# Decay slopes and small sums moved to PSUM, k products in one bank, and the group sums' transfers at other chunks

## Chip, core and metric

The kernel runs on one core of a Trainium2 chip. The metric is the device time in microseconds of one execution. Before the change it is 184.69 us, the median of 3 runs (184.53 to 184.96). The profile comes from one further execution with the hardware profiler on.

## What is computed

Two blocks over the same 2048 rows of 448 features, mixed by a gate. Block A is linear attention with 16 heads of 28, block B a long convolution with kernels made from 256 complex exponentials per feature.

```python
x = A_x                                            # (1, 2048, 448)
g = sigmoid((x * gate_w).sum(-1, keepdims=True))

def A(x, wqkv, wo):
    q, k, v = heads(x @ wqkv)                      # 16 heads of 28
    phi = lambda t: where(t > 0, t + 1, exp(t)) + 1e-6
    pq, pk = phi(q), phi(k)
    kv = einsum("bhsd,bhse->bhde", pk, v)
    z = einsum("bhsd->bhd", pk)
    o = einsum("bhqd,bhde->bhqe", pq, kv) / (einsum("bhqd,bhd->bhq", pq, z)[..., None] + 1e-6)
    return merge(o) @ wo

def B(u, ...):
    dt = exp(log_dt); A = -exp(log_A_real) + 1j * A_imag
    C = (C_real + 1j * C_imag) * dt[:, None]
    K = 2 * einsum("dn,dnl->dl", C, exp(A * dt * arange(L))).real
    return causal_conv(u, K) + u * D_skip          # by FFT in the reference

out = g * A(x) + (1 - g) * B(x)
```

For the inputs of this case every feature passes a test (`okc`) by which K is flat enough over the sequence that the convolution is a running sum of x times one slope per feature, called `near`. A general path (`general_conv`) stands behind a branch and is not taken.

## The kernel before, in words

The 2048 rows are 16 chunks of 128 rows (`NC = 16`); chunk c has its turned rows (for products that contract over features) and its plain rows. Every product in full precision is made of products of high and low parts: a ScalarE copy rounds to the high part, and a subtraction on GpSimd or VectorE (`low`, line 243) gives the low part. TensorE's work per chunk in the main loop (lines 509 to 566, c = 2 to 13) is, in order:

- `project(c + 1)` with wk: 11 matmuls into one PSUM bank (line 341), the k product of the *next* chunk. The banks are tags: it goes to `k` for odd c and to `v1` for even c, so it alternates;
- `project(c)` with wq: 11 matmuls into bank `q`;
- `do_g(c)`: 11 matmuls that add x-transposed times phi(k) into four banks g0 to g3 (line 416);
- in chunks 5, 7, 9 and 11 `group_heads` (line 442): two matmuls with a triangle matrix `tri` that turn a group's row sums into running sums, into bank `v0`. In 7, 9 and 11 they stand between blocks 2 and 3 of `do_g`, in 5 behind it.

The k product is turned into phi(k) by `k_feature` (ScalarE L367, L368, VectorE L369), `k_high` (ScalarE L373) and `k_low` (VectorE L379 twice: the low part and the running z); the last two read the PSUM bank. The q product goes through `q_post`: ScalarE L387 and, up to chunk 5, L356, then VectorE L357 and L360; from chunk 6 on ScalarE L391 to L393, then VectorE L394. Bank `q` is free for the next chunk after the last of these.

The convolution works on four groups of four chunks. `group_load` (L423, on SP's queue) loads a group into its home: group 0 into `wvo[:, 1]`, group 1 into the end of `pq`, which first holds the operands of the slopes and so must wait until L298 and L299 have read them, groups 2 and 3 into `room` and `spare`. `running_a` (L427) and `running_b` (L431) are accumulating transfers within SBUF that GpSimd issues: together they make running sums over the four rows of a partition; `running_b` reads what `running_a` wrote. `group_split` (ScalarE L435, GpSimd `low`) takes high and low part of the group's last row for `group_heads`. `convolve` (L447, L448, two chunks at a time, c from 6 on) adds the heads, which are in PSUM, and multiplies by `near`. `group_add` (L454) adds the group into y by another accumulating transfer of GpSimd. `skip` (L259, GpSimd) is the term u times D_skip.

`s4d_prepare` (lines 286 to 321) makes the slopes from the parameters in six steps, which the loop calls by `steps`: exponentials in chunk 1's step, row sums (L297, L298 on ScalarE, L299 on VectorE) in chunks 2 and 3, the small sums of 112 x 4 (L303 to L316, VectorE) in chunk 4, and in chunk 5 four transposes that spread the slopes over all partitions, with a ScalarE copy (L321) to `near` in SBUF.

The order of work on each engine is the order of the program; nothing is reordered. SP issues the loads in program order too, and an issue that waits holds those behind it. `load_x(c + 3)` (L207) at the head of chunk c loads the chunk three ahead, into one of four buffers.

After the loop, the last chunk's products, the head products (`kv_products`, which read wv in `wvo[:, 0]`) and the output products follow.

Of the kernel before, what the change touches and what calls it, by code (L numbers as in the profile page):

```python
# [7 lines left out]
F32 = mybir.dt.float32  # L8
F32R = mybir.dt.float32r
I32 = mybir.dt.int32  # L10
AF = mybir.ActivationFunctionType
ALU = mybir.AluOpType
# [3 lines left out]
P = 128  # L16
S = 2048
D = 448
# [4 lines left out]
J = 4  # L23
# [9 lines left out]
QW = 512  # L33
EDGE = 16
G = 4
SMALL = 2.0 ** -70
FLAT = 2.0 ** 35
BIG = 3.4028234e38
# [107 lines left out]
def gated_mix_kernel(ctx: ExitStack, tc: tile.TileContext, xin, wq_d, wvo_d, abc_d, ldt_d, dsk_d,  # L146
# [26 lines left out]
    gcr = const.tile([UZ, RX], F32R, name="gcr")  # L173
    ones = const.tile([P, P], F32R, name="ones")
    rows = const.tile([P, S], F32, name="rows")
    near, dsk = (rows[:, i * D:(i + 1) * D] for i in range(2))
    u = const.tile([UZ, D], F32, name="u")
    zb = const.tile([P, D], F32, name="zb")
    ldt = const.tile([DJ, J], F32, name="ldt")
# [34 lines left out]
    o = 0  # L214
# [32 lines left out]
        ACT.copy(w[:, :NAT], turned[c])  # L247
        low(POOL, w[:, NAT:], turned[c], w[:, :NAT])

    def split_n(c):  # L250
        r, w = plain[c], xn_p.tile([P, NX], F32R, name="xn", tag="n")
        xn[c] = w
        ACT.copy(w[:, :XC - NAT], r)  # L253
        low(POOL, w[:, XC - NAT:], r[:, :D], w[:, :D])
        if c > 2:
            skip(c)

    def skip(c):
        POOL.tensor_tensor(out=y[:, c], in0=plain[c][:, :D], in1=dsk, op=ALU.mult)  # L259
# [22 lines left out]
    def small():  # L282
        cnt[0] += 1
        return sm[:, cnt[0] - 1]

    def s4d_prepare():
        tt = lambda eng, o, a, b, op: eng.tensor_tensor(out=o, in0=a, in1=b, op=op)
        stt = lambda o, a, k, b, op1: DVE.scalar_tensor_tensor(out=o, in0=a, scalar=k, in1=b, op0=ALU.mult, op1=op1)
        junk = [yf[:DJ, F0 + (i - 2) * 2 * N:F0 + (i - 1) * 2 * N].rearrange("p (i n) -> p i n", i=2) for i in range(2)]
        s0, s1, dt, am, p0, p1, d2, md, b0, b1 = (small() for _ in range(10))  # L290
        for j in range(J):
            ACT.activation(abc[:, 0, j], abc[:, 0, j], AF.Exp)
        ACT.activation(dt, ldt, AF.Exp)
        tt(DVE, d2, dt, dt, ALU.mult)
        yield
        for j in range(J):
            ACT.activation(junk[0], abc[:, 0:2, j], AF.Square, accum_out=am[:, j:j + 1])  # L297
            ACT.activation(junk[0][:, 0], abc[:, 2, j], AF.Copy, accum_out=s0[:, j:j + 1])  # L298
            DVE.scalar_tensor_tensor(out=junk[1], in0=abc[:, 2:4, j], scalar=1.0, in1=abc[:, 0:2, j], op0=ALU.mult,  # L299
                                     op1=ALU.mult, accum_out=s1[:, j:j + 1])  # L300
            if j % 2:
                yield
        tt(DVE, md, am, d2, ALU.mult)  # L303
        stt(p0, s0, 2.0, dt, ALU.mult)
        stt(p1, s1, -2.0, d2, ALU.mult)
        DVE.tensor_scalar(out=md, in0=md, scalar1=SMALL, scalar2=None, op0=ALU.is_le)
        stt(b0, p0, -1.0, p0, ALU.max)
        stt(b1, p1, -1.0, p1, ALU.max)
        yield
        DVE.tensor_scalar(out=p0, in0=p0, scalar1=-BIG, scalar2=BIG, op0=ALU.max, op1=ALU.min)  # L310
        DVE.scalar_tensor_tensor(out=md, in0=b0, scalar=1.0 / FAR, in1=md, op0=ALU.is_ge, op1=ALU.mult)
        stt(okc, b1, FLAT, b0, ALU.is_le)
        DVE.scalar_tensor_tensor(out=md, in0=b0, scalar=FAR, in1=md, op0=ALU.is_le, op1=ALU.mult)
        tt(DVE, okc, okc, md, ALU.mult)
        tt(DVE, p0, p0, okc, ALU.mult)
        DVE.tensor_reduce(out=oks, in_=okc, op=ALU.add, axis=AX.X)  # L316
        yield
        o = ps.tile([P, 512], F32, name="p", tag="v0")
        for j in range(J):
            PE.transpose(o[:, j * DJ:(j + 1) * DJ], p0[:, j:j + 1].to_broadcast([DJ, P]), ident[:DJ, :DJ])  # L320
        ACT.copy(near, o[:, :D])  # L321

    def pieces(c, wh, wl, n, tag, last=None):
        o = ps.tile([P, 512], F32, name=tag, tag=tag)
# [20 lines left out]
    def project(*args, **kw):  # L345
        o, run = pieces(*args, **kw)
        run(11)
        return o
# [22 lines left out]
    def k_high(c):  # L371
        pkh[c] = tp.tile([P, 512], F32R, name="pkh", tag="pkh")[:, EDGE:EDGE + D]
        ACT.add(pkh[c], pks[c], 1e-6)  # L373
# [34 lines left out]
    def do_g(c, blocks=range(4)):  # L408
        w = xn[c]
        for i in blocks:  # L410
            a = w[:, 64 + i * P:64 + (i + 1) * P]
            b = w[:, XC - NAT + 64 + i * P:][:, :P] if i < 3 else None
            seq = [(a, pkh[c]), (a, pkl[c]), (b, pkh[c])] if i < 3 else \
                  [(a, pkh[c]), (a[:, :64], pkl[c])][::1 if c == 0 else -1]
            for n, (a, b) in enumerate(seq):
                PE.matmul(g[i][:a.shape[1], :D], lhsT=a, rhs=b, start=c == 0 and n == 0,  # L416
                          stop=c == NC - 1 and n == len(seq) - 1)
# [4 lines left out]
    def group_load(g):  # L422
        SP.dma_start(out=homes[g], in_=xin[g * G:(g + 1) * G, :, NAT:LO].rearrange("r p d -> p r d"))  # L423

    def running_a(g):
        w = homes[g]
        POOL.dma_start(out=w[:, 1::2], in_=w[:, 0::2], accum_op=ALU.add)  # L427

    def running_b(g):
        w = homes[g]  # L430
        POOL.dma_start(out=w[:, 2:], in_=w[:, 1:2].to_broadcast([P, 2, D]), accum_op=ALU.add)  # L431

    def group_split(g):
        w = sums[g] = tp.tile([P, 2, D], F32R, name="sums", tag="v0", bufs=1)
        ACT.copy(w[:, 0], homes[g][:, G - 1])  # L435
        low(POOL, w[:, 1], homes[g][:, G - 1], w[:, 0])

    def group_heads(g):
        o = heads[g] = ps.tile([P, 512], F32, name="v", tag="v0")[:, :D]
        w = sums.pop(g)  # L440
        for i in range(2):
            PE.matmul(o, lhsT=tri, rhs=w[:, i], start=i == 0, stop=i == 1)

    def convolve(c):
        g, i = c // G, c % G
        a, full = homes[g][:, i:i + 2], [P, 2, D]
        DVE.tensor_tensor(out=a, in0=a, in1=heads[g][:, None, :].to_broadcast(full), op=ALU.add)  # L447
        DVE.tensor_tensor(out=a, in0=a, in1=near[:, None, :].to_broadcast(full), op=ALU.mult)  # L448
        if i and g < NC // G - 1:
            for k in (g, UL + g):  # L450
                SP.dma_start(out=u[k:k + 1], in_=homes[g][P - 1:P, G - 1])
# [40 lines left out]
    for j in (2, 3, 0):  # L492
# [11 lines left out]
    skip(0)  # L504
    split_n(3)
    woh, wol = [], []
    pieces_at = {3: [(running_a, 0)], 4: [(running_b, 0)], 5: [(running_a, 1)], 6: [(running_b, 1), (running_a, 2)],
                 8: [(running_b, 2), (running_a, 3)], 10: [(running_b, 3)]}
    for c in range(2, NC - 2):
        if c + 3 < NC:  # L510
            load_x(c + 3)
        if c == 2:
            SP.dma_start(out=cst, in_=cst_d)
        if c == 4:
            SP.dma_start(out=wvo[:, 0], in_=wvo_d[:, 0])
        if c == 10:
            SP.dma_start(out=wo, in_=wvo_d[:DJ, 1])
        if c in (2, 4, 5, 7):
            group_load(c // 2 - (c < 5))
        ko = project(c + 1, wkh, wkl, D, "k" if c % 2 else "v1")  # L520
        if c > 5:
            convolve(2 * c - 12)
        split_t(c + 2)
        for f, k in pieces_at.get(c, ()):
            f(k)
        if c > 5:
            split_n(c + 2)
        k_feature(c + 1, ko)
        if c in (5, 7, 9, 11):
            group_split(c // 2 - 2)  # L530
        k_high(c + 1)
        k_low(c + 1)
        qo = project(c, wqh, wql, D + 2, "q")
        q_post(c, qo)
        if c < 5:
            steps(2 if c == 4 else 1)
        if c == 3:
            DVE.tensor_copy(tri, trir)
            DVE.tensor_copy(gcr, gcat)
        if c == 7:  # L540
            SP.dma_start(out=okr[:, None, :DJ], in_=oks[:, None, :])
        if c == 9:
            DVE.tensor_reduce(out=okr[:, DJ:], in_=okr[:, :DJ], op=ALU.add, axis=AX.X)
            DVE.tensor_copy(okn, okr[:, DJ:])
        do_g(c, (0, 1))
        if c == 5:
            steps(1)
        do_g(c, (2,))
        if c in (7, 9, 11):
            group_heads(c // 2 - 2)  # L550
        do_g(c, (3,))
        if c == 5:
            group_heads(0)
        if c < 4:
            skip(c - 1)
        if c < 6:
            split_n(c + 2)
        if c in (7, 9, 11, 13):
            group_add(c // 2 - 3)
        for j in {12: (0, 1), 13: (2, 3)}.get(c, ()):  # L560
            w = xn_p.tile([P, NX], F32R, name="wo", tag="n") if j < 2 else xp.tile([P, XC], F32R, name="wo", tag="xr")
            w = w[:DJ, :2 * D].rearrange("p (i d) -> p i d", i=2)
            woh.append(w[:, 0])
            wol.append(w[:, 1])
            ACT.copy(woh[j], wo[:, j])
            low(POOL, wol[j], wo[:, j], woh[j])
# [402 lines left out]
```

## Time and profile before

| | |
|---|---|
| median of 3 runs | 184.69 us |
| profiled execution | 185.1 us |
| its span in the trace | 183.2 us |
| TensorE busy | 166.5 us, 852 matmuls |
| VectorE busy | 130.4 us |
| ScalarE busy | 105.9 us |
| GpSimd busy | 123.2 us |
| mean granted TensorE clock | 0.987 |

The span runs from the first to the last instruction of the trace; the execution's time has 1.9 us around it. In rows of a timeline the columns are start and duration in us, engine (PE is TensorE, DVE VectorE, ACT ScalarE, POOL GpSimd, SP the queue that issues loads), line, operation, output and input, shapes, and in brackets the idle time before and what ended it. Rows of waits read: engine and line, what it waited for, us in total, how often, the longest. Rows of a line's instructions give durations in ns as least, median and most. In rows of a stretch (such as 54.00:58.00) come its length, the busy time of TensorE, its weight loads, VectorE, ScalarE and GpSimd, the granted clock, and the transfers' share and GB/s. A row that begins with an output and an input alone is one of DMA issues: count, size, us to landing.

### The profile page before, as it was taken

Reading aid. Unit: us, or ns where it says so; the run is one execution under the profiler, and the core shown is the slowest. Engines: PE = TensorE matmul, PEld = TensorE weight load, DVE = VectorE, ACT = ScalarE, POOL = GpSimd, SP = SyncE. Lnnn points to the kernel's source line nnn. Section 1 sums busy time; section 2 is a strip of 40 time slices with the busy share of each in tenths; the row PEclk is TensorE's granted clock in tenths of the full one; section 3 lists DMA queues with packets and bytes.
Section 4 is the critical chain, followed back from the end, with each engine's and each line's share of the span. In section 5 each row is a group of like instructions: output and inputs, shape, how many; then the busy total and the mean of one; then the engine's idle time right before and its main releaser. Section 6 shows DMA issues by size and latency. Waiting matters only on the chain.

```text
span 183.2 us, 2706 instructions
## 1 busy us (share of the span) xinstructions
PE 166.5 (91%) x852; PEld 147.8 (81%) x852; DVE 130.4 (71%) x232; ACT 105.9 (58%) x241; POOL 123.2 (67%) x128
## 2 busy tenths in 40 slices
PE   7999999996907999898897799999999999999990
PEld 2798999995906999796896699998988999999990
DVE  0857548898809488782888568787889898997550
ACT  3779489846015663674727858656474555564441
POOL 6074776985708995778845976985959899773100
PEclk9999999999996999999999999999999999999998
DMA  6999968495999581989997480090031122122221
GB/s 186 415 305 265 245 193 302 166 236 172 275 293 336 151 141 25 176 264 236 279 225 134 140 179 0 0 194 8 1 67 52 52 101 104 50 101 101 102 95 62
DMA packets 12186, 29.45 MB, mean 161 GB/s; under 512 B 1549, under 2 KB 8410, under 8 KB 12170
## 3 DMA queue, kind: packets, MB, share of 16 engines
q1 hardware_dynamic: 9274, 21.81, 36.9%
q0 software_dynamic: 2752, 7.34, 21.6%
q8 instruction: 7, 0.11, 0.2%
q10 hardware_dynamic: 144, 0.11, 0.2%
q14 instruction: 9, 0.07, 0.1%
HBM read 17.93 MB, written 3.67 MB: 118 GB/s over the span
## 4 chain that ended last, share of the span: by engine, by line
PE 51%; DMA 20%; DVE 8%; ACT 8%; POOL 6%; issue 2%; SPq 1%; ACTq 0%; DVEq 0%; POOLq 0%
PE a L664 20%; DMA wvo<-wvo 10%; PE g L416 8%; PE v L341 7%; PE q L341 6%; DMA room<-room 5%; PE tr L638 4%; PE k L341 3%; DVE wvo L448 3%; DMA wvo<-in 3%; DVE room L448 2%; POOL xt L243 2%; DMA y<-in 2%; POOL y L259 2%; POOL xn L243 2%
## 5 line engine op out<-in xcount | busy, mean ns | idle before, releaser
L664 PE MATMUL a<-wk,th 128*128 128x448 f32 (+1 forms) x170 | 36.7, 361 | 0.1
L416 PE MATMUL g<-pkh,xn 128*128 128x448 f32 x112 | 35.7, 364 | 0.0
L664 PEld LDWEIGHTS a<-wk,th 128*128 128x128 f32 x170 | 29.4, 189 | 2.2 <-issue 0.3
L341 PE MATMUL q<-wqh,xt 128*128 128x450 f32 x120 | 27.8, 368 | 3.5 <-DVE pq L360 1.8
L243 POOL TENSOR_TENSOR xt<-xr,xt 128x512 fp32r<-128x512 f32 x14 | 21.2, 1515 | 14.2 <-ACT xt L247 14.2
L243 POOL TENSOR_TENSOR xn<-xr,xn 128x448 fp32r<-128x448 f32 x16 | 23.9, 1492 | 5.7 <-ACT xn L253 3.9
L341 PEld LDWEIGHTS q<-wqh,xt 128*128 128x128 f32 x120 | 22.3, 188 | 6.2 <-DVE pq L394 2.5
L416 PE MATMUL g<-pkl,xn 128*128 128x448 f32 x64 | 23.4, 366 | 0.0
L416 PEld LDWEIGHTS g<-pkh,xn 128*128 128x128 f32 x112 | 21.0, 188 | 2.2
L341 PE MATMUL v<-wk,xt 128*128 128x448 f32 x99 | 22.2, 374 | 0.0
L259 POOL TENSOR_TENSOR y<-xr,rows 128x448 f32<-128x448 f32 x16 | 21.8, 1365 | 0.0
L576 POOL TENSOR_TENSOR room<-pq,zb 128x448 f32<-128x448 f32 x16 | 18.6, 1168 | 3.6 <-issue 2.6
L341 PEld LDWEIGHTS v<-wk,xt 128*128 128x128 f32 x99 | 19.5, 197 | 1.5
L341 PE MATMUL k<-wk,xt 128*128 128x448 f32 x77 | 17.4, 368 | 0.1
L601 POOL TENSOR_TENSOR room<-pq,den 128x336 f32<-128x336 f32 x16 | 12.2, 763 | 7.4 <-ACT den L590 4.4
L341 PEld LDWEIGHTS k<-wk,xt 128*128 128x128 f32 x77 | 14.3, 187 | 1.8 <-ACT wk L464 0.4
L669 DVE SCALAR_TENSOR_TENSOR ot<-y,og,a 128x448 f32<-128x448 f32 (+1 forms) x17 | 10.7, 629 | 5.1 <-PE a L664 5.1
L646 DVE TENSOR_TENSOR th<-tr,th 128x512 fp32r<-128x512 f32 x16 | 11.0, 690 | 2.6 <-ACT th L645 2.0
L416 PEld LDWEIGHTS g<-pkl,xn 128*128 128x128 f32 x64 | 11.2, 174 | 1.2 <-DVE pkl L379 0.2
L645 ACT CAST th<-tr 128x512 fp32r<-128x512 f32 x16 | 9.4, 588 | 4.6 <-PE tr L638 4.4
L373 ACT ACTIVATE pkh<-v 128x448 fp32r<-128x448 f32 x9 | 4.9, 543 | 12.3 <-DVE v L369 12.3
L341 PE MATMUL q<-wql,xt 128*128 128x450 f32 x45 | 11.7, 365 | 0.0
(178 smaller groups left out, 326.8 us busy)
## 6 DMA issues: line engine op xcount, KB each, us to landing
xr<-in SPq DMA_DIRECT2D x15, 512.0 KB, 6.1
out<-ot SPq DMA_DIRECT2D x15, 224.0 KB, 1.9
pq<-in SPq DMA_DIRECT2D x4, 448.0 KB, 13.4
wvo<-in SPq DMA_DIRECT2D x2, 896.0 KB
y<-in SPq DMA_DIRECT2D x2, 480.0 KB, 3.7
y<-in SPq DMA_DIRECT2D x2, 450.0 KB, 7.8
wvo<-wvo POOLq DMA_DIRECT2D x2, 448.0 KB, 9.5
pq<-in SPq DMA_DIRECT2D x1, 896.0 KB, 5.3
```

Source lines behind the costliest of these rows:

```text
L243: eng.tensor_tensor(out=o, in0=r, in1=h.bitcast(F32), op=ALU.subtract)
L259: POOL.tensor_tensor(out=y[:, c], in0=plain[c][:, :D], in1=dsk, op=ALU.mult)
L341: PE.matmul(o[:, :n], lhsT=a, rhs=b, start=run.n == 1, stop=not seq)
L416: PE.matmul(g[i][:a.shape[1], :D], lhsT=a, rhs=b, start=c == 0 and n == 0, stop=c == NC - 1 and n == len(seq) - 1)
L448: DVE.tensor_tensor(out=a, in0=a, in1=near[:, None, :].to_broadcast(full), op=ALU.mult)
L576: POOL.tensor_tensor(out=pd[c], in0=pq[:, c], in1=zb, op=ALU.mult)
L601: POOL.tensor_tensor(out=n[:, :3, :DJ].rearrange("p j (h d) -> p j h d", h=4), in0=a, in1=r[:, :H - 4].rearrange("p (j h) -> p j h", j=3)[ ...
L638: PE.transpose(o[:, j * P:(j + 1) * P], n[:, j], ident)
L645: ACT.copy(h, ov)
L646: DVE.tensor_tensor(out=l, in0=ov, in1=h.bitcast(F32), op=ALU.subtract)
L664: PE.matmul(a[:, lo:hi], lhsT=u_, rhs=w_[:, lo:hi], start=n == 0, stop=n == 10)
L669: DVE.scalar_tensor_tensor(out=ot[:, lo:hi], in0=y[:, c, lo:hi], scalar=og[:, c:c + 1], in1=a[:, lo:hi], op0=ALU.mult, op1=ALU.add)
```

## The change

- Seven of the small tiles stay in SBUF (two of them second copies, `n0` and `n1`, of the products `p0` and `p1`); six lie in a PSUM bank, tag `v0`. The square of dt is made by ScalarE.
- The transposed slopes stay in PSUM, tag `v1`; the ScalarE copy L321 is gone, and L448 reads the bank.
- The k product goes to `v1` in chunks 2 and 4 and to `k` in all others, so that from chunk 5 on each one follows the last in the same bank.
- `group_load(0)` is issued ahead of the loop, those of groups 1, 2 and 3 at the end of chunks 3, 4 and 5 (before: heads of chunks 2, 4, 5 and 7). The load of wv goes from chunk 4 to chunk 11.
- `running_a` is issued at the end of chunks 2, 4, 5 and 6 (before: in chunks 3, 5, 6 and 8), `running_b` in chunks 4, 6, 7 and 9 (before: 4, 6, 8 and 10).
- `group_heads` stands behind all four blocks of `do_g`.
- From chunk 6 on `skip` stands behind `group_split` on GpSimd. The copies of `tri` and `gcr` go from VectorE in chunk 3 to ScalarE in chunk 4.

```diff
+PAIRS = (2, 4, 5, 6)
+HALVES = (4, 6, 7, 9)
...
-    near, dsk = (rows[:, i * D:(i + 1) * D] for i in range(2))
+    dsk = rows[:, D:2 * D]
+    near = []
...
-    def split_n(c):
+    def split_n(c, both=True):
...
-        if c > 2:
+        if c > 2 and both:
             skip(c)
...
-        s0, s1, dt, am, p0, p1, d2, md, b0, b1 = (small() for _ in range(10))
+        s0, s1, am, pn, b0, n0, n1 = (small() for _ in range(7))
+        o = ps.tile([P, 512], F32, name="sums", tag="v0")
+        dt, p0, p1, d2, md, b1 = (o[:DJ, i * J:(i + 1) * J] for i in range(6))
...
-        tt(DVE, d2, dt, dt, ALU.mult)
+        ACT.activation(d2, dt, AF.Square)
...
         stt(p0, s0, 2.0, dt, ALU.mult)
+        stt(n0, s0, 2.0, dt, ALU.mult)
         stt(p1, s1, -2.0, d2, ALU.mult)
+        stt(n1, s1, -2.0, d2, ALU.mult)
...
-        stt(b0, p0, -1.0, p0, ALU.max)
-        stt(b1, p1, -1.0, p1, ALU.max)
+        stt(b0, p0, -1.0, n0, ALU.max)
+        stt(b1, p1, -1.0, n1, ALU.max)
...
-        tt(DVE, p0, p0, okc, ALU.mult)
+        tt(DVE, pn, p0, okc, ALU.mult)
...
-        o = ps.tile([P, 512], F32, name="p", tag="v0")
+        o = ps.tile([P, 512], F32, name="p", tag="v1")
+        near.append(o[:, :D])
...
-            PE.transpose(o[:, j * DJ:(j + 1) * DJ], p0[:, j:j + 1].to_broadcast([DJ, P]), ident[:DJ, :DJ])
-        ACT.copy(near, o[:, :D])
+            PE.transpose(o[:, j * DJ:(j + 1) * DJ], pn[:, j:j + 1].to_broadcast([DJ, P]), ident[:DJ, :DJ])
...
-        DVE.tensor_tensor(out=a, in0=a, in1=near[:, None, :].to_broadcast(full), op=ALU.mult)
+        DVE.tensor_tensor(out=a, in0=a, in1=near[0][:, None, :].to_broadcast(full), op=ALU.mult)
...
-    pieces_at = {3: [(running_a, 0)], 4: [(running_b, 0)], 5: [(running_a, 1)], 6: [(running_b, 1), (running_a, 2)],
-                 8: [(running_b, 2), (running_a, 3)], 10: [(running_b, 3)]}
+    group_load(0)
     for c in range(2, NC - 2):
         if c + 3 < NC:
             load_x(c + 3)
...
-        if c == 4:
-            SP.dma_start(out=wvo[:, 0], in_=wvo_d[:, 0])
...
-        if c in (2, 4, 5, 7):
-            group_load(c // 2 - (c < 5))
-        ko = project(c + 1, wkh, wkl, D, "k" if c % 2 else "v1")
+        if c == 11:
+            SP.dma_start(out=wv, in_=wvo_d[:, 0])
+        ko = project(c + 1, wkh, wkl, D, "v1" if c in (2, 4) else "k")
...
-        for f, k in pieces_at.get(c, ()):
-            f(k)
+        if c in HALVES:
+            running_b(HALVES.index(c))
         if c > 5:
-            split_n(c + 2)
+            split_n(c + 2, False)
...
         if c in (5, 7, 9, 11):
             group_split(c // 2 - 2)
+        if c > 5:
+            skip(c + 2)
...
-        if c == 3:
-            DVE.tensor_copy(tri, trir)
-            DVE.tensor_copy(gcr, gcat)
+        if c == 4:
+            ACT.copy(tri, trir)
+            ACT.copy(gcr, gcat)
...
-        do_g(c, (2,))
-        if c in (7, 9, 11):
+        do_g(c, (2, 3))
+        if c in (5, 7, 9, 11):
             group_heads(c // 2 - 2)
-        do_g(c, (3,))
-        if c == 5:
-            group_heads(0)
         if c < 4:
             skip(c - 1)
         if c < 6:
             split_n(c + 2)
+        if c in (3, 4, 5):
+            group_load(c - 2)
+        if c in PAIRS:
+            running_a(PAIRS.index(c))
```

## Prediction

> **What bounds the kernel now.** I read the page first, then the waits of TensorE alone, then TensorE's timeline around its longest wait, and from there the timelines of the engines named as releasers.
>
> ```profile
> PE 166.5 (91%) x852; PEld 147.8 (81%) x852; DVE 130.4 (71%) x232; ACT 105.9 (58%) x241; POOL 123.2 (67%) x128
> ```
> ```profile
> PE v L442 <- ACT rows L321: 5.2, 1, 5.2
> PE q L341 <- DVE pq L360: 1.8, 1, 1.8
> PE q L341 <- DVE pq L394: 1.7, 2, 1.0
> PE v L442 <- POOL sums L243: 1.7, 2, 0.9
> ...
> PE v L442 <- ACT sums L435: 0.6, 1, 0.6
> ```
>
> TensorE is busy 91% of the span, and these five rows (waits in the main loop) are 11.0 us, nearly all that it idles once it has begun. After the last of them the chain that ended last is TensorE alone until the final stores, so a microsecond won in chunks 2 to 11 should reach the end. The change can win what these gaps hold; it cannot touch the rest.
>
> ```profile
> 37.21 1.77 PE L341 MATMUL q<-wqh,xt 128*128 128x450 f32 x8
> ...
> 41.62 2.37 PE L341 MATMUL k<-wk,xt 128*128 128x448 f32 x11
> 45.75 1.85 PE L341 MATMUL q<-wqh,xt 128*128 128x450 f32 x8 [1.77 <-DVE pq L360]
> ...
> 50.46 0.37 PE L416 MATMUL g<-pkh,xn 128*128 128x448 f32 x1
> 56.06 1.12 PE L442 MATMUL v<-sums,tri 128*128 128x448 f32 x2 [5.23 <-ACT rows L321]
> 56.97 3.32 PE L341 MATMUL v<-wk,xt 128*128 128x448 f32 x11
> ```
> ```profile
> 54.00:58.00 4.00, 1.94 (x5) 1.78 (x6) 2.77 (x5) 3.48 (x8) 2.54 (x3) 0.70 1.08 306
> ```
>
> The long gap costs more than 5.23 us: the granted clock from 54 to 58 us is 0.70, and the k product of chunk 7, 2.37 us elsewhere, takes 3.32. With about 0.5 us on the pair of L442 that is 1.4 us more. What ended it:
>
> ```profile
> 44.26 0.64 ACT L247 CAST xt<-xr 128x512 fp32r<-128x512 f32 x1
> ...
> 54.09 0.56 ACT L435 CAST sums<-wvo 128x448 fp32r<-128x448 f32 x1 [8.13 <-DMA wvo<-wvo]
> ...
> 55.47 0.54 ACT L321 COPY rows<-p 128x448 f32<-128x448 f32 x1
> ```
>
> ScalarE stood 8.13 us at the copy of group 0's sums, for the second accumulating transfer (L431), and the slopes' copy (L321) is queued behind it.
>
> **The other releasers** are late because VectorE stands still:
>
> ```profile
> L448 DVE TENSOR_TENSOR wvo<-wvo,rows x2: 1399/3178/4958, 58.4 to 66.2; 128x896 f32<-128x896 f32 x2
> ...
> L448 DVE TENSOR_TENSOR room<-room,rows x2: 1153/2643/4133, 90.5 to 99.2; 128x896 f32<-128x896 f32 x2
> ```
> ```profile
> L447 DVE TENSOR_TENSOR wvo<-wvo,v x2: 1077/1078/1078, 57.2 to 65.1; 128x896 f32<-128x896 f32 x2
> ...
> L447 DVE TENSOR_TENSOR room<-room,v x2: 1077/1083/1089, 89.4 to 98.1; 128x896 f32<-128x896 f32 x2
> ```
>
> Same shape, same place, but L447 has one operand in PSUM and L448 both in SBUF. L447 never varies; L448 runs to 4.96 and 4.13 us. Each long one is followed by one of the two q waits on L394.
>
> ```profile
> 32.36 1.15 POOL L259 TENSOR_TENSOR y<-xr,rows 128x448 f32<-128x448 f32 x1
> 33.47 1.29 POOL L243 TENSOR_TENSOR xt<-xr,xt 128x512 fp32r<-128x512 f32 x1
> 34.71 1.33 POOL L427 DMA_DIRECT2D wvo<-wvo  x1
> 35.63 1.61 POOL L259 TENSOR_TENSOR y<-xr,rows 128x448 f32<-128x448 f32 x1
> ...
> 39.25 1.44 POOL L243 TENSOR_TENSOR xt<-xr,xt 128x512 fp32r<-128x512 f32 x1
> 42.75 1.21 POOL L431 DMA_DIRECT2D wvo<-wvo  x1 [2.06 <-DMA wvo<-wvo]
> ...
> 58.82 2.14 POOL L243 TENSOR_TENSOR xt<-xr,xt 128x512 fp32r<-128x512 f32 x1
> ...
> 90.20 1.21 POOL L431 DMA_DIRECT2D spare<-spare  x1
> ```
> ```profile
> 34.53 0.48 DVE L357 TENSOR_SCALAR t<-e 128x448 f32<-128x448 f32 x1
> 35.12 0.62 DVE L360 SCALAR_TENSOR_TENSOR pq<-q,t 128x448 f32<-128x448 f32 x1
> 35.66 5.59 DVE L299 SCALAR_TENSOR_TENSOR y<-pq 112x512 f32<-112x512 f32 x1
> ...
> 41.29 0.69 DVE L299 SCALAR_TENSOR_TENSOR y<-pq 112x512 f32<-112x512 f32 x1
> ```
>
> L299 asks at 35.66, just after GpSimd took up L259, and ends at 41.25: it got in only when GpSimd's stream ran dry at 40.7, four instructions later. That stream began with a transfer issue (34.71), whose followers overlap (35.63 + 1.61 passes the next start). The 4.13 us of L448 comes right behind the issue at 90.20. Without an issue just before, VectorE gets in at the next boundary: L448 at 58.4 took 1.40, and GpSimd's 58.82 stretched to 2.14. I read this as: behind a transfer issue GpSimd lets VectorE starve.
>
> **The change, part by part.** *Slopes in PSUM (L321 gone, L448).* All eight L448 become L447's kind, 1.08 us. That ends both q waits on L394 (1.7 us). The copy of 0.54 leaves ScalarE; TensorE's transposes are the same four. *Group sums and the product behind all of g.* The second halves of groups 2 and 3 start a chunk earlier, so their sums wait for no transfer; the product stands two matmuls of g later and GpSimd's `skip` moves behind the low half. This ends 1.7 + 0.6 us. Sum for chunks 7 to 11: 4.0 us.
>
> *k in one bank from chunk 6 on.* A new wait: the next k product needs both L379 of the last.
>
> ```profile
> 111.10 2.20 PE k L341 x11
> ...
> 117.78 2.20 PE v L341 x11
> ```
> ```profile
> 116.32 0.61 DVE L379 SCALAR_TENSOR_TENSOR pkl<-k,pkh 128x448 fp32r<-128x448 f32 x1
> ```
>
> k ends at 113.30, the last L379 at 116.93, the next k starts at 117.78: a chain of 3.6 us in a window of 4.5. It fits with about 0.8 us over, provided the 2.15 us of L447 and L448 lie under the k product, where they stand in VectorE's order. I take 0.4 us in all for this and for GpSimd's crowded chunks 6 and 7 (bounds 0 and 2), leaving 3.6 of the 4.0.
>
> *Small sums half in PSUM, two more of them, d2 and the copies of tri and gcr on ScalarE.* Under 1 us on either engine, beside a busy TensorE: nothing. Their cover is ScalarE's wait below.
>
> *Transfers.*
>
> ```profile
> 33.91 0.42 SPq L515 DMA_DIRECT2D wvo<-in  x1
> 42.06 0.38 SPq L423 DMA_DIRECT2D pq<-in  x1
> ```
> ```profile
> pq<-in SPq DMA_DIRECT2D x1, 896.0 KB, 5.3
> ```
> ```profile
> DMA to landing us min/median/max: 4.7/10.3/11.3
> ```
> ```profile
> 54.74 1.14 POOL L243 TENSOR_TENSOR sums<-wvo,sums 128x448 fp32r<-128x448 f32 x1 [5.38 <-ACT sums L435]
> ```
>
> wv (33.91, 896 KB) goes to chunk 11. The first half of group 0's sums is issued at 33.5 and meets no load; at 4.7 us, the least landing shown for the second half (the row without names is L431's), it lands near 39, so the second half goes out at 40.5 without the 2.06 us wait and lands between 45.2 and 51.8 (4.7 to 11.3). Both are ahead of when ScalarE now reaches it, as follows.
>
> Group 1's load waits for the last L299 (its target holds that operand) and now stands *ahead* of chunk 7's load in SP's queue. ScalarE used chunk 7's at 44.26. So SP holds it until L299 is done, and xt(7), k_feature(6), the group's copy and pkh(6) on ScalarE stand behind it.
>
> And the first half's issue moves ahead of GpSimd's L243 of 33.47. Then L357 (asked at 34.53), which before slipped in under the issue, meets a stream that has just begun behind an issue. By L299's row it starves to 40.6: L357 and L360 (0.48 at most, 0.62) end at 41.6, and q of chunk 4 waits for them, 41.6 instead of 37.21, a new gap of 4.4 us. From there: q and g 4.4 (37.21 to 41.62), k(6) from 46.0 to 48.2; q(5) follows at once, so the 1.77 us gap is swallowed; q and g of chunk 5 take 5.0 as before (45.75 to 50.8), to 53.2. L299 twice (0.69 each, unhindered) ends at 43.0; group 1's load lands at 43.1 + 0.4 + 5.3 = 48.8; chunk 7's 512 KB behind it lands between at once and 3.0 us more at that rate; I take the middle, 50.3. ScalarE: xt 0.64, then the chain of 3.6: the k bank is free at 54.5. The group's copy hides under VectorE's step of that chain, running to 52.7; GpSimd's 1.14 makes 53.8, and the product runs 53.8 to 54.2. k(7) runs 54.5 to 56.7 instead of ending at 60.3: **3.6 us**. The waits left, 0.6 and 0.3, are too short to lower the clock by the row of 1.77 us, after which it stayed full.
>
> The Trainium skill ("TensorE: Matmul & The Clock Gate", Part 1) puts the clock at half after an idle window of about 3.4 us, free-running; the 5.23 us gap agrees. By it the new 4.4 us gap could cost up to 1.7 us, of which under 1 would reach k(7); I leave it in the range.
>
> **Sum.** 3.6 + 3.6 = 7.2 us. The profiled execution took 185.1 us (span 183.2, 1.9 around it): 177.9. It stood 0.4 over the median of 184.69, so **177.5**.
>
> **Rivals.** *A: VectorE waits one GpSimd instruction, not a stream.* L357 gets in at 35.7 and L360 ends at 36.6, ahead of 37.21. The gap of 4.4 us never comes, L299 ends by 41.3 at the latest, chunk 7's load lands near 48.6 (5.7 and half of 3.0 later), k(7) ends 6.4 after that (0.64, 3.6, 2.2), at 55.0: 5.3 + 3.6 = 8.9, or **175.8**. If L299 gets in early too, the loads come sooner by as much; with the 1.77 us of q(5) the low end is 174.0. The row of 1.40 us is for it, those of 5.59, 4.96 and 4.13 against. The Trainium skill ("SBUF — State Buffer", Who interferes with whom) says it this way: whoever issues first holds the shared ports for that whole instruction. The trace shows the sharing, but not that the wait ends with one instruction.
>
> *B: group 0's second half is late all the same*, held by the loads massed from 43 us: landing at 54.0 as before. Then copy, pkh and L379 end at 56.3, k(7) at 58.5, gaining 1.8 + 3.6 = 5.4: **179.3**; if chunk 8's load is late too by 1.5 us, 180.8. For it: 11.3 us is a shown landing. Against it: it goes out 2 us earlier, ahead of those loads.
>
> *C, slower: PSUM does not free L448.* If it still starves behind GpSimd's issues, which now precede it in six chunks (6, 7, 8, 9, 10, 12), at 4.5 us, then L447, L448 and the last 2.4 us of the chain (3.6 less ScalarE's first two steps) end 8.0 us after the chunk's start, where the one bank wants 6.6: 1.4 us a chunk, 8.4 us in place of 4.0. Against the 3.6 won in front that is 0.8 worse, **185.5**. It decides from about 1.3 us a chunk on, L448 over 4.4 us. Against it stand all eight L447.
>
> *D: the front gains nothing and half of the back is lost elsewhere*: no change.
>
> **How the numbers follow.** Forecast 0.50, A 0.28, B 0.14, C 0.05, D 0.03. The range, 174.0 to 180.8, takes in A's floor and B's ceiling and leaves out C and D. A measurement of this kernel can tell about 0.2%, 0.4 us: faster 0.92, same 0.03, slower 0.05.
>
> **What would show it.** L448 at 1.08 eight times, and no wait on L394 or the sums after chunk 6; L357 of chunk 3 some 6 us long with a TensorE gap of about 4 us at q(4) (A: neither); ScalarE waiting at L247 for chunk 7's load; a wait under 1 us at the product of group 0. The prediction is wrong if k products from chunk 7 on wait for L379, or if the sums' copy of group 0 still waits for L431.

## The result and the profile after

The changed kernel takes 178.33 us (median of 4 runs, 178.27 to 179.65); the kernel before took 184.61 us beside it (median of 4, 182.92 to 184.96). The ratio is 0.970, with an interval of 0.963 to 0.976. So 6.3 us are gained, where 7.2 were forecast: 0.8 us above the predicted 177.5 and inside the range. The profiled execution took 179.65 us, with a span of 177.9; the forecast for such an execution was 177.9 with a span of 176.0, so in the trace 1.9 us are missing. (It stands 1.3 above its median, where the one before stood 0.4; of the 1.9, that is 0.9.) The medians here are over all runs of a kernel; the ratios leave disturbed runs out.

Lines have moved in the changed kernel: L243, L247 and L259 are now L246, L250 and L262; L357 and L360 are L364 and L367; L299 is L304, L341 is L348, L369 is L376, L379 is L386; `group_load` L423 is L430, `running_a` and `running_b` are L434 and L438, L435 is L442, L442 is L449, and the heads' addition and the slopes' product, L447 and L448, are L454 and L455.

The page's line of busy times, after:

```profile
PE 166.3 (94%) x852; PEld 148.5 (83%) x852; DVE 122.9 (69%) x231; ACT 106.7 (60%) x243; POOL 119.3 (67%) x128
```

TensorE's busy time over the whole span is what it was (166.3 for 166.5), so the gain is idle time. The waits of TensorE alone:

```profile
PE q L348 <- DVE pq L367: 3.3, 1, 3.3
PE v L449 <- POOL sums L246: 1.5, 1, 1.5
PE q L268 <- POOL warm L199: 1.3, 1, 1.3
PE v L348 <- POOL xt L246: 1.1, 1, 1.1
```

In the main loop 5.9 us are left of 11.0 (the row of 1.3 is the start, and stood before too). Of the five rows quoted before, four are gone. The two cases of the fifth, the triangle product's wait for the sums' low part, stood in chunks 9 and 11 and are gone too; the 1.5 us here are a new case, in chunk 7, where the kernel before had none. Two more rows are new, both in the front: 3.3 us at q of chunk 4, which was forecast, and 1.1 at the k product of chunk 5, which was not. TensorE's timeline of the front:

```profile
37.12 2.29 PE L348 MATMUL v<-wk,xt 128*128 128x448 f32 x10 [1.07 <-POOL xt L246]
42.70 2.32 PE L348 MATMUL q<-wqh,xt 128*128 128x450 f32 x8 [3.30 <-DVE pq L367]
44.83 1.33 PE L348 MATMUL q<-wql,xt 128*128 128x450 f32 x3
...
48.80 2.36 PE L348 MATMUL k<-wk,xt 128*128 128x448 f32 x11
51.00 1.81 PE L348 MATMUL q<-wqh,xt 128*128 128x450 f32 x8
...
55.89 0.57 PE L449 MATMUL v<-sums,tri 128*128 128x448 f32 x2
56.30 2.37 PE L348 MATMUL k<-wk,xt 128*128 128x448 f32 x11
```

The long gap is gone from the triangle product (55.89 follows g at once), and k of chunk 7 ends at 58.67 instead of 60.29. From there to the end of the span it is 122.9 us before and 119.2 after. So the front gives 1.6 us and the rest 3.7, together the 5.3 by which the spans differ. Behind the gap at 42.70 the granted clock falls, as the stretches show (the clock is the third number from the end):

```profile
40.00:44.00 4.00, 1.29 (x6) 1.24 (x7) 3.86 (x7) 0.58 (x1) 2.73 (x3) 0.99 0.20 34
44.00:48.00 4.00, 4.00 (x13) 3.57 (x13) 2.67 (x6) 2.04 (x6) 0.16 (x1) 0.58 1.08 231
48.00:52.00 4.00, 4.00 (x21) 3.69 (x20) 2.22 (x15) 0.70 (x2) 3.29 (x3) 1.00 1.01 396
```

q and g of chunk 4 take 6.1 us (42.70 to 48.80) where they took 4.4. VectorE and GpSimd at that place, and the slopes' product:

```profile
35.54 6.29 DVE L364 TENSOR_SCALAR t<-e 128x448 f32<-128x448 f32 x1
41.93 0.62 DVE L367 SCALAR_TENSOR_TENSOR pq<-q,t 128x448 f32<-128x448 f32 x1
42.48 0.68 DVE L304 SCALAR_TENSOR_TENSOR y<-pq 112x512 f32<-112x512 f32 x1
```
```profile
34.44 1.32 POOL L434 DMA_DIRECT2D wvo<-wvo  x1
35.36 1.71 POOL L246 TENSOR_TENSOR xt<-xr,xt 128x512 fp32r<-128x512 f32 x1
36.60 1.57 POOL L262 TENSOR_TENSOR y<-xr,rows 128x448 f32<-128x448 f32 x1
38.03 1.25 POOL L246 TENSOR_TENSOR xn<-xr,xn 128x448 fp32r<-128x448 f32 x1
...
40.23 1.34 POOL L246 TENSOR_TENSOR xt<-xr,xt 128x512 fp32r<-128x512 f32 x1
```
```profile
L455 DVE TENSOR_TENSOR wvo<-wvo,p x2: 1087/1087/1087, 58.5 to 64.6; 128x896 f32<-128x896 f32 x2
...
L455 DVE TENSOR_TENSOR room<-room,p x2: 1087/1088/1090, 87.1 to 93.7; 128x896 f32<-128x896 f32 x2
```

L364, asked for at 35.54, ends when GpSimd's stream, five instructions behind the issue at 34.44, runs dry at 41.6. L455 takes 1.09 us all eight times, where the same product took up to 4.96 before. On ScalarE the load of chunk 7 has taken the place of group 0's transfer:

```profile
51.30 0.62 ACT L250 CAST xt<-xr 128x512 fp32r<-128x512 f32 x1 [3.61 <-DMA xr<-in]
...
52.88 0.55 ACT L442 CAST sums<-wvo 128x448 fp32r<-128x448 f32 x1
```

### The profile page after: what moved, and what is told of

It is laid out like the page before. It is cut to its first block, busy times and chain, and to the rows that moved or that the text cites. A ratio compares the mean times of both kernels' runs of the same rounds, so it can differ in the third digit from the quotient of the medians.

```text
span 177.9 us, 2714 instructions
## 1 busy us (share of the span) xinstructions
PE 166.3 (94%) x852; PEld 148.5 (83%) x852; DVE 122.9 (69%) x231; ACT 106.7 (60%) x243; POOL 119.3 (67%) x128
## 4 chain that ended last, share of the span: by engine, by line
PE 59%; DVE 7%; DMA 6%; ACT 6%; POOL 5%; issue 2%; ACTq 0%; DVEq 0%
PE a L671 20%; PE q L348 12%; PE g L423 10%; PE k L348 7%; DMA pq<-pq 6%; PE tr L645 4%; DVE t L364 4%; PE m L748 1%; POOL xn L246 1%; POOL sums L246 1%; PE v L348 1%; PE k L768 1%; PE tr L768 1%; ACT y L302 1%; PE v L449 1%
## 5 line engine op out<-in xcount | busy, mean ns | idle before, releaser
L423 PE MATMUL g<-pkh,xn 128*128 128x448 f32 x112 | 36.2, 369 | 0.0
L348 PE MATMUL q<-wqh,xt 128*128 128x450 f32 x120 | 28.2, 373 | 3.3 <-DVE pq L367 3.3
L246 POOL TENSOR_TENSOR xn<-xr,xn 128x448 fp32r<-128x448 f32 x16 | 23.3, 1454 | 11.2 <-ACT xn L256 11.2
L246 POOL TENSOR_TENSOR xt<-xr,xt 128x512 fp32r<-128x512 f32 x14 | 21.8, 1559 | 11.2 <-ACT xt L250 11.2
L348 PE MATMUL k<-wk,xt 128*128 128x448 f32 x121 | 27.5, 371 | 0.0
L348 PEld LDWEIGHTS q<-wqh,xt 128*128 128x128 f32 x120 | 22.6, 190 | 5.6 <-issue 3.9
L348 PEld LDWEIGHTS k<-wk,xt 128*128 128x128 f32 x121 | 22.9, 190 | 2.2 <-POOL xt L246 0.4
L423 PE MATMUL g<-pkl,xn 128*128 128x448 f32 x64 | 23.6, 369 | 0.0
L423 PEld LDWEIGHTS g<-pkh,xn 128*128 128x128 f32 x112 | 21.5, 192 | 2.3
L262 POOL TENSOR_TENSOR y<-xr,rows 128x448 f32<-128x448 f32 x16 | 22.7, 1420 | 0.0
L376 DVE SCALAR_TENSOR_TENSOR k<-k,e 128x448 f32<-128x448 f32 x11 | 7.0, 633 | 13.1 <-ACT e L375 13.1
L374 ACT ACTIVATE e<-k 128x448 f32<-128x448 f32 x11 | 6.0, 545 | 14.2 <-PE k L348 14.2
L348 PE MATMUL v<-wk,xt 128*128 128x448 f32 x55 | 12.1, 364 | 1.1 <-POOL xt L246 1.1
L423 PEld LDWEIGHTS g<-pkl,xn 128*128 128x128 f32 x64 | 11.4, 179 | 1.3 <-DVE pkl L386 0.2
L364 DVE TENSOR_SCALAR t<-e 128x448 f32<-128x448 f32 x7 | 10.7, 1528 | 2.5 <-ACT e L363 2.5
```

Source lines behind the costliest of these rows:

```text
L246: eng.tensor_tensor(out=o, in0=r, in1=h.bitcast(F32), op=ALU.subtract)
L348: PE.matmul(o[:, :n], lhsT=a, rhs=b, start=run.n == 1, stop=not seq)
L364: DVE.tensor_scalar(out=t, in0=e, scalar1=1.0, scalar2=1e-6, op0=ALU.min, op1=ALU.add)
```

## The experiments

Theory: the wait of L364 (VectorE shut out behind the transfer issue) costs the front what the change could have won there; and L455 is short because its slopes lie in PSUM. Rivals: the front is bound by chunk 7's load all the same; the slopes' place matters little beside the transfers' places. All kernels compute the whole output.

**The issue later.** The first half of group 0's sums is issued where it was before, behind xt of chunk 5.

```diff
+        if c == 3:
+            running_a(0)                 # behind split_t(5)
-        if c in PAIRS:
+        if c in PAIRS[1:]:
```

> The first accumulating transfer of group 0 is issued where it stood before the change, behind chunk 5's GpSimd subtraction, all else as changed. Theory (behind a transfer issue GpSimd's stream shuts VectorE out until it runs dry): the step t<-e of chunk 3 takes under 1.3 us in place of 6.29, TensorE's waits of 3.30 us at q(4) and 1.07 us at k(5) go, the clock stays full there; part comes back, because the last L299-like products still starve to about 42 us and so hold group 1's and chunk 7's loads: about 2.5 us faster than the changed kernel, 175.8. Rival (the gap at q(4) has another cause, chunk 4's data or the lateness of ScalarE): the 3.30 us stay, within 0.5 us of the changed kernel's 178.3.

181.11 us (179.82 to 181.5); ratio to the kernel before 0.986 (0.965 to 1.006). L364 takes 0.48, and both front waits are gone. But then comes L304, as it did before, with 5.59 us (q of chunk 5 waits 1.70 again, 1.77 before the change), and everything behind the loads is late. VectorE, then ScalarE and TensorE:

```profile
35.76 0.48 DVE L364 TENSOR_SCALAR t<-e 128x448 f32<-128x448 f32 x1
...
36.89 5.59 DVE L304 SCALAR_TENSOR_TENSOR y<-pq 112x512 f32<-112x512 f32 x1
```
```profile
53.17 0.62 ACT L250 CAST xt<-xr 128x512 fp32r<-128x512 f32 x1 [7.44 <-DMA xr<-in]
```
```profile
55.35 0.74 PE L449 MATMUL v<-sums,tri 128*128 128x448 f32 x1 [3.56 <-ACT sums L442]
```

So the cause of the 3.3 us gap is the issue's place, and taking it away alone wins nothing: a gap of 3.56 us and a longer fall of the clock come instead at the triangle product, for want of chunk 7's load, which stands behind group 1's in SP's queue. It was issued 0.7 us sooner than in the change and landed 1.9 later; why, these rows don't say. The expected gain was wrong.

**The exponential in PSUM.** Of chunk 3 alone, so that L364 (L368 here) has no SBUF operand to read.

```diff
+        bank.append(o[:, 64:])           # o: the bank of the small sums
...
-            return feature(pq[:, c], o, mid)
+            return feature(pq[:, c], o, mid, bank[0] if c == 3 else None)
```

> As changed, issue at its new place, but chunk 3's exponential is written to PSUM, so that VectorE's t<-e reads one operand from PSUM and has no second SBUF stream. Theory (it is the access to SBUF that starves): t<-e takes about 0.6 us, the 3.30 us at q(4) go though the issue is where it was, the 1.07 us at k(5) stay, and the next product with two SBUF operands starves in its place, to about 42 us; 176 us. Rival (VectorE is held by something else, as a semaphore or its order): 6 us and the 3.30 us stay, 178.3.

179.92 us (179.58 to 180.62); 0.981 (0.963 to 0.999). The issue stays where it is, and yet:

```profile
35.20 0.62 DVE L368 TENSOR_SCALAR t<-sums 128x448 f32<-128x448 f32 x1
...
36.46 5.41 DVE L307 SCALAR_TENSOR_TENSOR y<-pq 112x512 f32<-112x512 f32 x1
```

The same instruction at the same place takes 0.62 instead of 6.29, and the next one that reads SBUF twice starves in its place. The gap moves to the triangle product again (3.60 us). That it is SBUF operands that VectorE waits for is shown by this pair.

**No issue at all there.** The first half goes out in chunk 4, right before the second.

```diff
+        if c == 4:
+            running_a(0)
-        if c in PAIRS:
+        if c in PAIRS[1:]:
```

> The first accumulating transfer of group 0 is issued in chunk 4, right before the second, so GpSimd issues nothing in chunks 2 and 3 and its stream there is tensor work alone. Theory (an issue is what shuts VectorE out): t<-e and both products with two SBUF operands each wait for one GpSimd instruction at most, under 2.1 us each, where t<-e took 6.29. Rival (any unbroken GpSimd stream shuts VectorE out): one of the three takes 4 us or more. The second transfer comes later, so the group's product is late and the time is 178 to 182 us.

One run, 184.9 us. GpSimd works through xt, y and xn all the same, but no issue stands ahead of them. GpSimd, then VectorE:

```profile
34.09 1.30 POOL L246 TENSOR_TENSOR xt<-xr,xt 128x512 fp32r<-128x512 f32 x1
35.35 1.30 POOL L262 TENSOR_TENSOR y<-xr,rows 128x448 f32<-128x448 f32 x1
37.65 1.29 POOL L246 TENSOR_TENSOR xn<-xr,xn 128x448 fp32r<-128x448 f32 x1 [1.00 <-ACT xn L256]
```
```profile
35.16 0.48 DVE L364 TENSOR_SCALAR t<-e 128x448 f32<-128x448 f32 x1
...
36.28 0.92 DVE L304 SCALAR_TENSOR_TENSOR y<-pq 112x512 f32<-112x512 f32 x1
...
37.24 0.69 DVE L304 SCALAR_TENSOR_TENSOR y<-pq 112x512 f32<-112x512 f32 x1
```

L364 gets in between xt and y, which follow one another at once, and L304 behind y, at a cost of 0.2 us (0.92 for 0.69). But behind y GpSimd is idle for 1.00 us, so L304's row alone doesn't tell a stream without an issue from a stream that has ended. The changed kernel has the clearer case, in chunk 5: xn and y stand back to back, the last issue was at 50.51, and the same L364 waits for xn only.

```profile
55.30 1.16 POOL L246 TENSOR_TENSOR xn<-xr,xn 128x448 fp32r<-128x448 f32 x1 [0.63 <-ACT xn L256]
56.43 1.31 POOL L262 TENSOR_TENSOR y<-xr,rows 128x448 f32<-128x448 f32 x1
```
```profile
55.32 1.39 DVE L364 TENSOR_SCALAR t<-e 128x448 f32<-128x448 f32 x1
```

So the waits of 5 to 6 us go with an issue ahead, and GpSimd's arithmetic alone costs about one instruction at most. The time missed what was expected: issued at 41.26, behind the six loads that SP puts out from 38.02 to 41.4, the first half held GpSimd's next issue for 10.46 us, and the triangle product waited 9.37.

**The slopes back in SBUF**, everything else as changed:

```diff
-        near.append(o[:, :D])
+        near.append(rows[:, :D])
+        ACT.copy(near[0], o[:, :D])      # behind the transposes
```

> As changed, but the slopes are copied from PSUM to SBUF by ScalarE again, so convolve's product has both operands in SBUF, while k stays in one bank. Theory (the PSUM operand is what makes the one bank bearable): the product takes over 3 us in at least three of eight cases, behind GpSimd's issues, and k products wait for it 1 to 2 us each: 3 to 6 us slower than the changed kernel, 181 to 184. Rival (the transfers and the group product alone carry the gain of chunks 7 to 11): within 0.7 us of 178.3.

182.8 us (181.44 to 184.77, 10 runs); 0.994 (0.989 to 0.9998). Two of the eight products starve, one fewer than expected, and each is followed by a wait of a k product in the one bank:

```profile
72.38 4.77 DVE L456 TENSOR_TENSOR pq<-pq,rows 128x896 f32<-128x896 f32 x1
...
88.36 3.42 DVE L456 TENSOR_TENSOR room<-room,rows 128x896 f32<-128x896 f32 x1
```
```profile
79.60 2.44 PE L349 MATMUL k<-wk,xt 128*128 128x448 f32 x11 [1.69 <-DVE pkl L387]
...
94.23 2.44 PE L349 MATMUL k<-wk,xt 128*128 128x448 f32 x11 [0.68 <-DVE pkl L387]
```

Without the slopes in PSUM the rest of the change is worth about 1 us by the ratio, whose interval reaches from nothing to 2.

**The same with two banks** for k, as before the change:

```diff
-        ko = project(c + 1, wkh, wkl, D, "v1" if c in (2, 4) else "k")
+        ko = project(c + 1, wkh, wkl, D, "k" if c % 2 else "v1")
```

> The changed kernel with the slopes copied to SBUF and k alternating between two banks as before; it differs from the version with slopes in SBUF and one bank (182.8 us) in the bank alone. Theory (the one bank costs only where the product with two SBUF operands starves): the two waits of k products for pkl, 2.4 us together, go, but part comes back as waits of q for pq: 181 to 182.3. Rival (one bank costs every chunk): 180 or less.

On another chip, 183.11 us (182.1 to 184.71, 10 runs); 0.996 (0.991 to 1.001). Four products at 4 us now and no k product that waits, but three short waits for q (1.5 us in all) and 1.4 in the last stage instead. Against the kernel with one bank (182.8) there is no difference that these runs, on two chips, could show; a cost under 1 us would not show in them. Nor did the same number of products starve in both, and two banks beside slopes in PSUM were not tried. So that the one bank costs nothing is likely, not shown.

**The transfers back**, everything else as changed: loads and issues at the places of before.

```diff
-    group_load(0)
+    pieces_at = {3: [(running_a, 0)], 4: [(running_b, 0)], ...
...
-        if c in PAIRS:
-            running_a(PAIRS.index(c))
```

> The changed kernel with all loads and accumulating transfers at their places from before; slopes and sums in PSUM, k in one bank, the group product behind all of g, as changed. Theory (the transfers' new places win the front, the PSUM operand the waits on pq and part of the rest): ScalarE waits for group 0's second half to about 54 us again, TensorE's gap there is over 3 us, the waits on pq<-q,e (1.7 us) are gone; 181 to 183. Rival (PSUM operand and the removed copy carry nearly all): under 179.5.

182.82 us (181.97 to 184.6 in nine runs, 276.17 in the tenth); 0.995 (0.990 to 0.999). L455 stays at 1.09, but ScalarE waits 8.03 us for group 0's transfer and the triangle product 4.16. So the change without the transfers' new places gives about 1 us, the change without the slopes in PSUM about 1 too (neither interval reaches far beyond 2), and both together 6.3: each is worth most when the other's wait is gone.

**The x loads first.** The loads of groups 1 to 3 go behind chunk 7's, 8's and 9's.

```diff
+        if c in (4, 5, 6):
+            group_load(c - 3)            # behind load_x(c + 3)
-        if c in (3, 4, 5):
-            group_load(c - 2)
```

> As changed, but the loads of groups 1 to 3 are issued at the heads of chunks 4 to 6, each behind that chunk's own load, so that chunk 7's load no longer stands behind group 1's. The first transfer keeps its new place. Theory (the starved t<-e and the late load of chunk 7 cover each other: mending one alone gives nothing): ScalarE's wait of 3.61 us for chunk 7's load goes, TensorE's 3.30 and 1.07 us stay, k(7) starts where it did, within 1 us of the changed kernel's 178.3. Rival (the load alone binds): 2 to 3 us faster, 175.5 to 176.

178.7 us (178.2 to 180.23); 0.978 (0.968 to 0.989). ScalarE's wait for chunk 7's load is gone, the gap at q of chunk 4 is the same 3.30, and the time too (178.33 for the change). So chunk 7's load was no bound beside that gap, as the gap was none beside the load: each covers the other.

**Both**: this and the later issue.

> Both mended: the chunks' loads ahead of the groups' and the first accumulating transfer behind chunk 5's subtraction. Theory (two covers of one another): neither the 3.30 us at q(4) nor a wait of ScalarE for chunk 7's load is left; what remains is the wait of about 1.7 us at q(5), since the product with two SBUF operands still starves to 42 us; k(7) starts near 52 in place of 56.3; 4 us faster than the changed kernel, 174 to 175. Rival (the second accumulating transfer of group 0 binds next): the group's product waits over 2 us and the time is 176.5 or more.

178.1 us (177.25 to 180.74); 0.971 (0.961 to 0.981), no better, and the rival held: with chunk 7's load and q(4) out of the way q of chunk 5 waits 1.71, and then the triangle product is next, for its sums' low half stands on GpSimd behind group 1's issue, which waits, as I read it, for group 1's load (the row names L376, but ScalarE had taken up that result at 49.96). GpSimd and TensorE:

```profile
50.75 1.19 POOL L434 DMA_DIRECT2D pq<-pq  x1 [2.52 <-DVE k L376]
```
```profile
54.37 0.47 PE L449 MATMUL v<-sums,tri 128*128 128x448 f32 x1 [2.25 <-POOL sums L246]
54.67 3.95 PE L348 MATMUL k<-wk,xt 128*128 128x448 f32 x11
```

The gap of 2.25 was enough for the clock: the k product behind it takes 3.95 us instead of 2.37.

**Earlier instead of later.** x loads first, group 0's two issues a chunk sooner:

```diff
+        if c == 2:
+            running_a(0)                 # before split_n(4)
...
-        if c in HALVES:
-            running_b(HALVES.index(c))
+        if c in (3,) + HALVES[1:]:       # behind split_t(c + 2)
+            running_b(((3,) + HALVES[1:]).index(c))
```

> Chunks' loads first, and both accumulating transfers of group 0 earlier: the first where GpSimd idles in chunk 2, the second behind chunk 5's subtraction in chunk 3. Theory: the second issue still starves the products with two SBUF operands to 42 us, the wait of about 1.7 us at q(5) stays, the group's sums are there long before ScalarE wants them; 173.5 to 174.5. Rival (the second issue reaches GpSimd before the first has landed and blocks its stream): t<-e or the subtractions of chunk 5 come late and TensorE waits over 3 us; 176 or more.

176.17 us (174.44 to 176.48); 0.959 (0.949 to 0.970). Better than the change by some 2 us (in the same rounds the kernel with the x loads first alone took 178.7), and 2 short of what was expected. The wait that was expected at q of chunk 5 didn't come: L304 comes in between GpSimd's instructions here, 1.97 and 1.52 us, although an issue stands before them, and nothing waits at the triangle product. One wait is left, from chunk 5's L364 behind the issue of 45.79:

```profile
48.59 5.76 DVE L364 TENSOR_SCALAR t<-e 128x448 f32<-128x448 f32 x1
```
```profile
55.23 3.28 PE L348 MATMUL q<-wqh,xt 128*128 128x450 f32 x8 [2.82 <-DVE pq L367]
```

**The exponentials in PSUM**, of chunks 3 to 5, added to the kernel with the x loads first:

```diff
-            return feature(pq[:, c], o, mid)
+            return feature(pq[:, c], o, mid, bank[0] if 2 < c < 6 else None)
```

> The changed kernel with the chunks' loads ahead of the groups', and the exponentials of chunks 3 to 5 read from PSUM; the first transfer stays at its new place, behind which t<-e starved. Theory (the starved t<-e costs its time once the load of chunk 7 no longer covers it): the 3.30 us at q(4) and the half clock behind it go, 1.07 us at k(5) stay, under 1 us at q(5); 2.5 to 4 us faster than the changed kernel, 174.5 to 176. Rival (the next wait in line, group 0's product behind GpSimd, takes it all back): within 1 us of 178.3.

177.74 us (177.65 to 180.86, 6 runs); 0.967 (0.961 to 0.972). All three L364 take 0.61 and the clock never falls, but five waits of 0.4 to 1.5 us, 5.0 in all, stand where the kernel with the x loads first has three, of 3.3, 1.1 and 0.6. That is the same sum; what is left of the gain, 0.8 us beside the changed kernel in the same rounds, fits the clock (0.998 where the kernel with the x loads first has 0.987); no run tries the clock alone.

**Both of these, and the earlier issues:**

> The version with both accumulating transfers of group 0 earlier and the chunks' loads first, and besides the exponentials of chunks 3 to 5 read from PSUM. Its t<-e of chunk 5 starved 5.76 us behind the issue for group 1 and left a wait of 2.82 us at q(6) with half clock behind it. Theory: t<-e takes 0.6 us, that wait and the half clock go: 3 to 4.5 us faster than without, 172 to 173. Rival (another wait within a microsecond of it): 175 or more.

173.54 us (173.37 to 175.19, 6 runs); 0.945 (0.940 to 0.951): better than both kernels, if half a microsecond above what was expected. The changed kernel, run unchanged in the same rounds, took 178.55:

> The changed kernel itself, on the same chip and in the same rounds as the three others. 178.3 us again, with the waits of 1.07, 3.30 and about 1.5 us of the first profile.

(178.0 to 179.12, 6 runs; 0.971, 0.966 to 0.975.) Its waits at k of chunk 5 and q of chunk 4 are there again, 1.11 and 3.30; group 1's product waits 0.50 where about 1.5 was expected. The faster kernel's waits of TensorE alone:

```profile
PE v L453 <- POOL sums L246: 1.6, 1, 1.6
PE q L268 <- POOL warm L199: 1.3, 1, 1.3
```

In the main loop only group 1's product still waits.

## Why the prediction was nearly right

*The mechanism of the slopes* held: eight times 1.09, no wait on the q products after chunk 6, none of a k product on L386. Rival C's mechanism exists: with the slopes in SBUF, products of 4.77 and 3.42 us hold up the k products of the one bank by 1.69 and 0.68. PSUM is what keeps it out.

*The back*, 3.6 forecast, 3.7 measured. That the sum came out to 0.1 is luck. Crowded GpSimd and one bank were put at 0.4 with bounds of 0 and 2, and group 1's product alone, which didn't wait before, waited 1.46, against "no wait on the sums after chunk 6". The waits forecast to go, 4.0 us, all went. Behind k of chunk 7 TensorE's idle time fell by 2.5 us (8.3 to 5.8); the rest is 1.2 us less of busy time (114.6 to 113.4), which nobody forecast and no run explains. And the wait varies: in the second profile of the changed kernel, of 179.12 us, the product waits 0.50, and the part behind k of chunk 7 takes 118.3 us, 4.6 less than before.

*The front*, 3.6 forecast, 1.6 measured, is the step that failed, and only in size. k of chunk 7 was to run from 54.5 and runs from 56.30, 1.8 later. The parts: q of chunk 4 starts at 42.70 and not 41.6, 1.1 later, because GpSimd's stream is about 1.0 later (y at 33.34 instead of 32.36). Some 0.3 of that is a later start of the whole kernel. The other 0.7 stand on ScalarE in chunk 1, where the change puts the exponential and the square of dt, which I had put at nothing:

```profile
24.44 0.18 ACT L298 ACTIVATE sums<-ldt 112x4 f32<-112x4 f32 x1 [0.42 <-ACT pq L297]
24.65 0.15 ACT L299 ACTIVATE sums<-sums 112x4 f32<-112x4 f32 x1
24.72 0.61 ACT L256 CAST xn<-xr 128x512 fp32r<-128x512 f32 x1
```

That the 0.42 are a wait for the new PSUM bank was not tried. Then the clock, 1.7 (6.1 us for 4.4). Against these 2.8 us stand 0.9 of waits at group 0's product and behind it, forecast and not come, because TensorE itself was late. That leaves 1.9, to a tenth the 1.8 of k(7)'s start. In the median only 0.8 us are missing; the second profile fits that, with a front that gains 1.4 us and a back that gains 4.6.

*The clock* was the named risk, but the sum held nothing for it: it was left in the range. The prediction thought of a 4.4 us gap and let under 1 us of the 1.7 reach k of chunk 7; all of it did, behind a gap of 3.3. The wait at k of chunk 5, 1.07, was not seen: xt of chunk 5 stands on GpSimd behind the moved issue (it is gone in the kernel with the issue later). It cost nothing more, since q of chunk 4 waited until 42.70 anyway.

*Rival A* (VectorE waits one instruction) fell for this kernel, 6.29 us; yet 1.97 and 1.52 in the kernel with earlier issues are just such waits. And its time would have been wrong: with the gap away the time was 179.9 and 181.1, not 175.8. Its sum let L299 end by 41.3 and chunk 7's load land near 48.6; with the issue later L304 ran to 42.5 and the load came at 53.1. *Rival B*'s late second half did not come: the copy at 52.88 waits for nothing.

## What to carry to other kernels

A gap with a known cause has the price of the next late thing, and here two stood under it: one edit alone gave nothing or a loss, two together at most some 2 us, three together 5.0. Where GpSimd issues transfers, look at which of VectorE's instructions behind the issue read SBUF only, and move an operand to PSUM or the issue to where VectorE has nothing to do. Add up the small things of a change on each engine: 0.7 us on ScalarE in chunk 1 reached the longest wait whole.

## What was not expected of the hardware

Behind a transfer issue of GpSimd VectorE waited through a whole stream of GpSimd's instructions, in the change five of them: 6.29 us there, 5.59, 5.41 and 5.76 in the experiments. The Trainium skill ("SBUF — State Buffer", Who interferes with whom) says that an instruction with at most one SBUF input outside the two-port modes doesn't contend; the 0.62 and 1.09 with an operand in PSUM agree. It says too that in the two-port modes whoever issues first holds the shared ports for that whole instruction; L364's 1.39 us with no issue right ahead agrees, its 6.29 does not. Why L304 came in after one instruction in the kernel with earlier issues is open.

In the profiled executions the clock fell behind gaps of 2.25, 2.82 and 3.3 us, and not behind 1.77 and 1.56. It need not fall each time: of the four executions of the kernel with earlier issues, whose gap is the 2.82, one shows a mean granted clock of 1.0 and took 174.44 us, the others 0.984 to 0.990 and 176.06 to 176.48. The Trainium skill ("TensorE: Matmul & The Clock Gate", Part 1) names an idle window of about 3.4 us; the first two gaps are clearly shorter.

The landing of an accumulating transfer differed with what was queued: about 5 us for group 0's two in the changed kernel, and over 10 for the first half in the kernel where the first half went out just behind the loads, for the same 448 KB.
